# Attention, then two feed-forward layers, under a list planner: a set-back for the attention sums, other staging buffers for the last matrix, two banks for layer one, and a new split of the last units

## The chip, the cores and the metric

The kernel runs on one core of a Trainium2 chip. The metric is the device time of one execution in microseconds (us). The runs shown of the kernel before have a median of 1149.49 us.

## The reference, cut to what matters

```python
scores = (1 / sqrt(64)) * q @ k.T                  # 4 batches, 8 heads, 576 tokens, 64 wide
kth    = 32nd largest score of each row
attn   = softmax(where(scores >= kth, scores, -1e9))
x      = (attn @ v), heads side by side            # 2304 tokens x 512
h      = x @ w_in;  g = max(0.01 * h, h)           # 512 -> 2048
y      = g @ w_out                                 # 2048 -> 512
m      = max(y @ w1, y @ w2, y @ w3)               # 512 -> 768, three times
out    = m @ w_out2                                # 768 -> 512
```

The weight matrices arrive as 64-bit floats, and the kernel turns them into pairs of 16-bit floats on the chip.

## The kernel before, in words

**Numbers.** Every operand of a matmul is kept as a high and a low 16-bit part, so each product is three matmuls (`three`, L873 to L876): high by high, high by low, low by high.

**Attention** (`attention`, L694). There are 72 steps in 20 blocks of up to 128 tokens; a step handles one block for two heads. Its parts, in their order, are: the scores on PE (L716, PSUM tile `s`, a part of `sav`), their copy to SBUF on ACT (L721, tile `S`, three buffers), the 32 largest values of each row on DVE (four MAX8 and three MATCH_REPLACE8 for each head, L736 and L738), the exponential on ACT (L786, `pp`), the mask on DVE and POOL (L791, L795, L798), the split into two 16-bit parts on ACT and POOL (L800, L802, `phl`), one transposing DMA on SP's queue (L805, `pt`), the product with v on PE (L831 to L833, tile `av`, the other part of `sav`), **the attention sums' addition on DVE (L838, `r`)** and their reciprocal (L840), four scaled copies on ACT (L842, `xs`), and the split of the result (`xhl`, L848 and L850). The tiles `pp`, `phl`, `pt`, `xs` and `xhl` have one buffer each. When a block is done, a transposing DMA (L868) puts its tokens into a **token buffer** `xu` (two buffers, handed out strictly in the order in which the program asks for them).

**Feed-forward** (`ffn`, L893). It runs over units of tokens, `UNITS` (L40). A unit can start when the last of its blocks has been attended. It has 672 matmuls of the unit's width: first layer (`h_tile`, L908, tiles `h<-xu,wi`; 16 tiles of 12 matmuls, one bank of the PSUM tag `h` each) and second layer (`acc<-f16t,wo`) interleaved, then the three matrices with their maximum (`h<-k,w`; the maximum is on DVE, L1015), interleaved with the last matrix (`acc<-f16t,w`). The tag `h` has four banks. The planner counts how many a phase may hold: `hH` for layer one, `hM` for the three matrices, `hW` for weight conversion.

**Weights** (`prep_w`, L469). Each chunk is loaded by SP (L484), converted on DVE by three operations for each piece (L498, L501, L504), measured on ACT (L344 or L519), scaled and split on ACT and POOL (L355 to L357). The chunks come in the order `w_in` (8), `w_out` (8), w1 to w3 (6), and the last matrix, called z (4, from `in_w2o`). z's chunks go through the two `raw` buffers, which also carry the loads of q, k and v of batches 1 to 3. A list `ZL` lets q, k and v of batches 2 and 3 wait for the last load of z, and z's loads wait for all q and k loads of batch 1. The conversion of z uses space that the three matrices' conversion used before it. All of z has to be there before the three matrices of unit 0 and before unit 1.

**Order of the work.** The program doesn't write instructions out in order. Each `op` becomes a node with an engine, an estimated duration, a priority `pr` and its dependencies, and `Plan.run` (L123) simulates the five engines: an engine takes the node that can start first, within a tolerance `eps`, and among those the one of lowest `pr`. What each engine executes is that order; on the chip it is fixed, and an instruction whose input is late holds up everything behind it on its engine. A node can start when its inputs are done plus a latency between engines:

```python
m.ready = max(m.ready, end + self.LAT.get((n.eng, m.eng), 0.2))
```

`GATES` (L467) makes chunks 1 and 2 of `w_in` and all chunks of w1 to w3 wait for a write of q of batch 0 to DRAM. `CVX` (L465) adds 0.06 us to the planned duration of a conversion that goes through PSUM.

Of the kernel before, what the change touches and what calls it, by code (L numbers as in the profile page):

```python
# [36 lines left out]
VC = 11  # L37
F0, F1, F2, F3, HB = (0, P), (P, P), (2 * P, P), (3 * P, P), (4 * P, 64)
ORDER = [[F0, HB, F1, F2, F3], [F0, F1, F2, F3, HB], [HB, F0, F1, F2, F3], [F0, F1, F2, F3, HB]]
UNITS = [192, 128] + [256] * 6 + [192, 256]  # L40

PE, ACT, DVE, POOL, SP = "PE", "ACT", "DVE", "POOL", "SP"

# [22 lines left out]


class Node:
    __slots__ = ("eng", "dur", "fn", "pr", "succ", "nd", "ready", "bufs", "eps", "idx", "dma")


class Plan:
# [10 lines left out]
        self.seqs[tag] += 1  # L83
        return b

    def op(self, eng, dur, fn, r=(), w=(), pr=0.0, dma=0.0):
        n = Node()
        n.eng, n.dur, n.fn, n.pr, n.dma = eng, dur, fn, pr, dma
        n.succ, n.ready, n.idx, n.eps = [], 0.0, len(self.nodes), self.eps
        deps, n.bufs = set(), []  # L90
        for k in r:
            if k in self.lastw:
                deps.add(self.lastw[k])
            self.readers.setdefault(k, []).append(n.idx)
        for k in w:
            deps.update(self.readers.get(k, ()))
            if k in self.lastw:
                deps.add(self.lastw[k])
        for k in w:
            self.lastw[k] = n.idx  # L100
            self.readers[k] = []
        deps.discard(n.idx)
        for k in list(r) + list(w):
            k = k[0] if isinstance(k, tuple) else k
            for b in (k, *k.also) if isinstance(k, Buf) else ():
                if b not in n.bufs:
                    n.bufs.append(b)
                    b.left += 1
                    b.emit += 1
        n.nd = len(deps)  # L110
        self.nodes.append(n)
        for d in deps:
            self.nodes[d].succ.append(n)
        return n
# [8 lines left out]
    def run(self):  # L123
        free = {e: 0.0 for e in (PE, ACT, DVE, POOL, SP)}
        dma_free = 0.0
        slots = {t: [0.0] * n for t, n in self.nbufs.items()}
        nexts = {t: 0 for t in self.nbufs}
        pend = {e: [] for e in free}
        order = []
        for n in self.nodes:  # L130
            if n.nd == 0:
                pend[n.eng].append(n)
        total = len(self.nodes)
        while len(order) < total:
            best = None
            for e, lst in pend.items():
                t0 = free[e]
                cand = None
                for n in lst:
                    t, ok = max(n.ready, t0), True  # L140
                    need = {}
                    for b in n.bufs:
                        if b.ap is None and b.last == 0.0 and not getattr(b, "on", False):
                            k = need.get(b.tag, 0)
                            sl = slots[b.tag]
                            if len(sl) <= k or (b.tag not in self.free_order and b.seq != nexts[b.tag] + k):
                                ok = False
                                break
                            need[b.tag] = k + 1
                            t = max(t, sl[k] + 0.2)  # L150
                    if not ok:
                        continue
                    key = (max(t - n.eps, t0), n.pr, n.idx)
                    if cand is None or key < cand[0]:
                        cand = (key, n, t)
                if cand is not None and (best is None or cand[2] < best[2]):
                    best = cand
            if best is None:
                raise RuntimeError("no instruction can go on")
            _, n, t = best  # L160
            pend[n.eng].remove(n)
            for b in n.bufs:
                if not getattr(b, "on", False):
                    b.on = True
                    slots[b.tag].sort()
                    slots[b.tag].pop(0)
                    nexts[b.tag] = max(nexts[b.tag], b.seq + 1)
            free[n.eng] = t + n.dur
            end = t + n.dur
            if n.eng == SP:  # L170
                st = max(t + 1.1, dma_free)
                dma_free = st + n.dma
                end = dma_free + 0.95
            order.append((t, n.idx))
            for b in n.bufs:
                b.left -= 1
                b.last = max(b.last, end)
                if b.left == 0:
                    slots[b.tag].append(b.last)
                    slots[b.tag].sort()  # L180
            for m in n.succ:
                m.nd -= 1
                m.ready = max(m.ready, end + self.LAT.get((n.eng, m.eng), 0.2))
                if m.nd == 0:
                    pend[m.eng].append(m)
        order.sort()
        for _, i in order if self.EMIT else ():
            n = self.nodes[i]
            for b in n.bufs:
                if b.ap is None:  # L190
                    b.ap = b.make()
            n.fn()
            for b in n.bufs:
                b.emit -= 1
                if b.emit == 0 and b.done:
                    b.done()
# [23 lines left out]
def attention_moe_kernel(ctx, tc, qk, v, w_in, w_out, w123, w2o, outT):  # L220
# [8 lines left out]

    NB = {"xu": 2, "raw": 2, "hl": 1, "k2": 7, "kt": 4, "qt": 2, "vt": 4, "S": 3, "w": 1, "m": 2, "nb": 2, "pp": 1,  # L230
          "phl": 1, "pt": 1, "r": 2, "xs": 1, "xhl": 1, "f16t": 4, "yj": 1,
          "s": 1, "av": 1, "acc": 2, "h": 4, "junk": 1, "xcap": 2, "pr": 8, "ph": 4, "ra": 3, "fi": 6, "ft": 9, "rw": 3, "fz": 3, "rc": 2, "hH": 3, "hM": 3, "hW": 1, "kH": 2, "kM": 5, "fH": 2, "fM": 2}
    PSUM_TAGS = ("s", "av", "acc", "h")
    plan = Plan(NB, {"raw", "av", "junk", "hl", "k2", "h", "f16t", "rc"})
    op = plan.op
# [2 lines left out]
    def buf(tag, shape, dt=F32):  # L238
        pl = ps if tag in PSUM_TAGS else sb

        def make():
            cnt[0] += 1
            if tag in ZONE:
                return ZONE[tag].pop(0)
            return pl.tile(shape, dt, tag=tag, bufs=NB[tag], name=f"{tag}_{cnt[0]}")

        b = plan.buf(tag, make)
        if tag in ZONE:
            b.done = lambda: ZONE[tag].append(b.ap)
        return b  # L250
# [106 lines left out]
        op(POOL, pool(n), lambda: G.tensor_tensor(lo(), src(), hi(), op=ALU.subtract), r=r + [w[0]], w=[w[1]], pr=pr)  # L357

    KT, QT, VT, ES = {}, {}, {}, {}
    ZL = [(("w", "z", 3), "ld")]  # L360

    def prep_qk(b, hp, pr, fast):
        d = dr.tile([2, 2, 2, D, S], F16, name=f"dqk{b}_{hp}")
# [96 lines left out]
        VT[b, hp] = t  # L460

    SC = {}
    CVK = "iotz"
    CW = 512
    CVX = 0.06  # L465
    PRW0 = -13.5
    GATES = {1: [("d", 0, 0, 0, 1)], 2: [("d", 0, 1, 0, 1)]}  # L467

    def prep_w(kind, c, parts, hi, lo, colnorm, n2c, s, bi, pr, tags, guard=((), (), []), gate=()):  # L469

# [6 lines left out]
        plan.eps = WEPS  # L477
        for i, saps in enumerate(parts):
            nf = sum(n for _, n in saps)
            f = buf(tags[1], [P, 768 if tags[1] == "raw" else 512], I32)  # L480
            o = 0
            for sap, n in saps:
                raw = buf(tags[0], [P, 768])
                op(SP, 0.55, lambda raw=raw, sap=sap, n=n: Y.dma_start(raw().bitcast(I64)[:, :n], sap),  # L484
                   w=[raw, (key, "ld")] + ([(f, "ld")] if tags[1] in ("raw", "k2") or tags[0] == "raw" else []),
                   r=list(gate) + zr + (zf + [("l1", hp, a) for hp in range(HP) for a in range(2)] * (kind == "z") + guard[2] * (tags[1] == "raw") if kind in "tz" else []), pr=PRW0 if (kind, c) == ("i", 0) else pr,
                   dma=dma(P * n * 8))
                for q in range(0, n, CW):
                    cw = min(CW, n - q)
# [70 lines left out]
    def c1(t, c):  # L560
        return t[:, c:c + 1]
# [25 lines left out]
                ["ZR"] if f < 3 else [("ZF", f - 2)]), gate=GATES[2])  # L587

    def w2_prep(e, pr):
        for hp in range(HP):  # L590
            if (1, hp) not in seen:
                seen.add((1, hp))
                prep_batch(1, hp)
        prep_w("z", e, [[(w2o[e, i], 384) for i in range(2)]], [w2[:, e, 0]], [w2[:, e, 1]],
               None, c1(cz, e), c1(sz, e), c1(bz, e), pr, ("raw", "fz" if e < 3 else "raw"),
               ({0: ["ZB"], 3: [("ZZ", 2)]}.get(e, []), [("ZZ", e - 1)] if e in (1, 2) else [],
                [("ZZ", e - 1)] if e else ["ZB"]))

# [77 lines left out]
        return TE + TS * i if i < NE else TA0 + TA * i  # L676

    EXPP = 4
    COLD = 1.7
    NCOLD = 8  # L680
    FM = 1
# [12 lines left out]
    def attention(i):  # L694
# [141 lines left out]
        nh = 2 if full else 4  # L836
        r = buf("r", [P, 8])
        op(DVE, 0.07, lambda: V.tensor_scalar(r()[:n, 0:nh].rearrange("p (x h) -> p x h", h=2),  # L838
                                             av()[:n, 0:nh // 2, :, 64], 1e-9 * PS, None, op0=ALU.add), r=[avb], w=[(r, 0)], pr=pr)
        op(DVE, 0.08, lambda: V.reciprocal(r()[:n, 4:4 + nh], r()[:n, 0:nh]), r=[(r, 0)], w=[(r, 1)], pr=pr)  # L840
        for h in range(nh):
            op(ACT, act(64, True, 1), lambda h=h: A.activation(xs()[:n, h], avh(h)[:n, 0:64], AF.Copy,  # L842
# [42 lines left out]
                (0, 2))  # L885

    MAXP = 40
    FINP = 40
    CS = 0.8
    DL = 99  # L890
# [2 lines left out]
    def ffn(u, pr0, between=None):  # L893
# [2 lines left out]
        xu = XU[u]  # L896
        xk = [(x, sg[2]) for sg in segs[u] for x in (xu, XC[u])]
        t3 = 3 * mm(N)
        acc, ak, ast, a0 = accs(N)
        clock = [pr0]  # L900

        def tick(t):
# [5 lines left out]
        def h_tile(f):  # L908
            pr = tick(1.3)
            c = f // (FCI // P)  # L910
            p = fbuf("h", "H", [P, 512])
            wk = wkeys("i", [c]) + wkeys("o", range(8)) * (u == 0) + wkeys("z", range(4)) * (u == 1)
            for k in range(KC):
                op(PE, t3, lambda k=k: three(p()[:, :N], lambda x: wi[:, x, k, f * P:(f + 1) * P],
                                             lambda x: xu()[:, x, k, :N], k == 0, k == KC - 1),
# [272 lines left out]
```

## Time and profile before

| what | value |
| --- | --- |
| runs shown, median (lowest to highest) | 1149.49 us (1147.88 to 1154.09), 3 runs |
| the profiled execution's own time | 1152.11 us |
| its span | 1150.2 us |
| mean granted TensorE clock | 0.96 |
| busy: PE, DVE, ACT, POOL | 912.4, 973.6, 757.3, 680.6 us |

The span is that of the program's instructions; 1.9 us of the execution lie around it. A busy share is an average over stages with different limits, so the stretches of the span have to be read apart: up to about 350 us weights are converted beside attention, until about 1050 us attention and feed-forward run side by side, and after that only feed-forward is left.

### The profile page before, as it was taken

What the parts mean: (1) busy time and instruction counts of PE and PEld (TensorE: products, weight loads), DVE (VectorE), ACT (ScalarE), POOL (GpSimd) and SP (SyncE); (2) the same over time, 40 slices, a digit from 0 to 9 for tenths busy, and PEclk for the clock granted to TensorE, in tenths of its full rate; (3) what the DMA queues carried; (4) which work ended last, traced back from release to release, by engine and by line L of the source; (5) the groups of instructions that cost most, each with busy time, mean ns of one, the idle gap of its engine ahead of it and who ended that gap; (6) DMA issues with size and microseconds to landing.
All of it is one profiled execution on the core that took longest, in us unless ns stands there. A gap on an engine that the chain in (4) does not pass through costs nothing.

```text
span 1150.2 us, 27408 instructions
## 1 busy us (share of the span) xinstructions
PE 912.4 (79%) x10294; PEld 797.7 (69%) x10294; DVE 973.6 (85%) x2154; ACT 757.3 (66%) x1625; POOL 680.6 (59%) x1054
## 2 busy tenths in 40 slices
PE   3253246853299799999899989989998998998998
PEld 2131235742199788887688778878887887898987
DVE  3989999989989999999899899899999999995001
ACT  7667747886457767567778665686786666665331
POOL 5555646875446766566777655575787556555231
PEclk9999998975599999999999999999999999999999
DMA  7758455654354423235574333364573433332000
GB/s 234 250 141 264 147 159 166 176 122 134 96 122 88 96 64 83 62 73 131 139 184 118 65 79 70 60 149 78 146 164 66 87 77 52 79 64 52 20 1 19
DMA packets 268549, 125.79 MB, mean 109 GB/s; under 512 B 237440, under 2 KB 255360, under 8 KB 266368
## 3 DMA queue, kind: packets, MB, share of 16 engines
q1 hardware_dynamic: 268416, 124.04, 44.6%
q8 instruction: 81, 1.33, 0.5%
q14 instruction: 52, 0.43, 0.1%
HBM read 62.65 MB, written 14.16 MB: 67 GB/s over the span
## 4 chain that ended last, share of the span: by engine, by line
PE 40%; DMA 14%; DVE 11%; POOL 7%; ACT 6%; issue 5%; SPq 1%; POOLq 0%; ACTq 0%; DVEq 0%
DMA pt<-phl 12%; PE h L874 7%; PE h L875 7%; PE h L876 7%; PE acc L875 4%; DVE m L736 4%; PE acc L874 4%; PE acc L876 4%; DVE w L738 3%; PE sav L716 3%; POOL phl L802 3%; PE sav L831 2%; PE sav L832 2%; PE sav L833 2%; POOL f16t L931 1%
## 5 line engine op out<-in xcount | busy, mean ns | idle before, releaser
L736 DVE MAX8 m<-w 128x8 f32<-128x576 f32 x432 | 309.7, 746 | 0.1
L931 POOL TENSOR_TENSOR f16t<-k,f16t 128x256 f16<-128x256 f32 (+2 forms) x220 | 142.8, 651 | 195.1 <-ACT f16t L925 184.1
L738 DVE MATCH_REPLACE8 w<-m,w 128x576 f32<-128x576 f32 x288 | 211.9, 741 | 0.0
L802 POOL TENSOR_TENSOR phl<-pp,phl 128x576 f16<-128x576 f32 x144 | 183.7, 1281 | 45.5 <-ACT phl L800 43.9
L874 PE MATMUL h<-k,w 128*128 128x256 f16 (+2 forms) x720 | 187.0, 264 | 7.8 <-ACT k L971 5.5
L875 PE MATMUL h<-k,w 128*128 128x256 f16 (+2 forms) x720 | 186.9, 264 | 3.7 <-POOL k L973 3.6
L876 PE MATMUL h<-k,w 128*128 128x256 f16 (+2 forms) x720 | 186.8, 264 | 0.0
L716 PE MATMUL sav<-kt,qt 128*128 128x288 f16 (+5 forms) x800 | 110.1, 288 | 77.1 <-ACT S L721 56.2
L875 PE MATMUL acc<-f16t,wo 128*128 128x256 f16 (+2 forms) x640 | 164.9, 262 | 4.7 <-POOL f16t L931 4.6
L874 PE MATMUL acc<-f16t,wo 128*128 128x256 f16 (+2 forms) x640 | 165.0, 262 | 0.0
L876 PE MATMUL acc<-f16t,wo 128*128 128x256 f16 (+2 forms) x640 | 165.0, 262 | 0.0
L874 PE MATMUL h<-xu,wi 128*128 128x256 f16 (+1 forms) x576 | 155.8, 270 | 5.0 <-ACT k L918 2.2
L876 PE MATMUL h<-xu,wi 128*128 128x256 f16 (+1 forms) x576 | 155.8, 271 | 0.0
L875 PE MATMUL h<-xu,wi 128*128 128x256 f16 (+1 forms) x576 | 155.8, 271 | 0.0
L800 ACT ACTIVATE phl<-pp 128x576 f16<-128x576 f32 x144 | 97.8, 681 | 65.0 <-DMA pt<-phl 27.8
L786 ACT ACTIVATE pp<-S,nb,colt 128x576 f32<-128x576 f32 x144 | 121.5, 860 | 20.6 <-POOL nb L776 12.7
L716 PEld LDWEIGHTS <-qt 128*128 128x128 f16 (+1 forms) x800 | 65.2, 109 | 99.8 <-issue 75.9
L798 POOL TENSOR_TENSOR pp<-pp,S 128x576 f32<-128x576 f32 x72 | 92.2, 1280 | 69.8 <-DVE S L795 42.9
L925 ACT ACTIVATE f16t<-k 128x256 f16<-128x256 f32 (+2 forms) x220 | 85.3, 392 | 59.9 <-DVE k L1015 57.2
L831 PE MATMUL sav<-vt,pt 128*128 128x65 f16 (+1 forms) x800 | 91.2, 202 | 38.5 <-DMA pt<-phl 34.1
L918 ACT ACTIVATE k<-h,colt 128x256 f32<-128x256 f32 (+2 forms) x160 | 71.1, 451 | 70.5 <-PE h L876 69.3
L721 ACT ACTIVATE S<-sav 128x576 f32<-128x576 f32 x144 | 92.8, 644 | 32.2 <-PE sav L716 18.4
(133 smaller groups left out, 2629.5 us busy)
## 6 DMA issues: line engine op xcount, KB each, us to landing
w<-in_w SPq DMA_DIRECT2D x18, 512.0 KB, 3.9
w<-in_w_in SPq DMA_DIRECT2D x8, 1024.0 KB, 6.6
w<-in_w_out SPq DMA_DIRECT2D x8, 1024.0 KB, 4.9
raw<-in_qk SPq DMA_DIRECT2D x24, 288.0 KB, 3.4
dqk<-hl SPq DMA_DIRECT2D x48, 144.0 KB, 2.5
kt<-dqk SPq DMA_DIRECT2D x16, 288.0 KB, 3.3
qt<-dqk SPq DMA_DIRECT2D x144, 32.0 KB, 2.2
raw<-in_v SPq DMA_DIRECT2D x12, 352.0 KB, 3.5
```

Of the source, the lines that this page charges most:

```text
L716: T.matmul(p()[osl, h, o:o + w], q()[:, hh, st, :n], k()[:, hh, kc:kc + w], start=st == 0, stop=st == 1, skip_group_check=True)
L721: op(ACT, act(S, True), lambda t=t, p=p: A.activation(t().rearrange("p (a s) -> p a s", a=2), p()[:, :, :288], AF.Copy), r=[p], w=[(Sp, j) ...
L736: op(DVE, dve(S) * 1.03, lambda mc=mc, src=src: V.max(mc(), src()), r=rd, w=[(m, j, 0, r)], pr=pd)
L738: op(DVE, dve(S) * 1.03 + 0.06, lambda mc=mc, src=src, j=j: V.match_replace(out=wj(j), in_to_replace=mc(), in_values=src(), imm_value=NEG) ...
L786: op(ACT, act(S, aps=2), lambda j=j, es=es: A.activation(pp()[:, j], Sb[j](), AF.Exp, bias=nb()[:, j:j + 1], scale=es[:, 0:1]), r=[(Sp, j) ...
L800: op(ACT, act(S), lambda j=j: A.activation(phl()[:, 0, j], pp()[:, j], AF.Copy), r=[(pp, j)], w=[(phl, 0, j)], pr=pr)
L802: op(POOL, pool(S), lambda j=j: G.tensor_tensor(phl()[:, 1, j], pp()[:, j], phl()[:, 0, j], op=ALU.subtract), r=[(pp, j), (phl, 0, j)], w= ...
L831: T.matmul(o, hc, vh, start=c == 0, stop=False, skip_group_check=True)
L874: T.matmul(out, wt(0), xt(0), start=first, stop=False, skip_group_check=True)
L875: T.matmul(out, wt(0), xt(1), start=False, stop=False, skip_group_check=True)
L876: T.matmul(out, wt(1), xt(0), start=False, stop=last, skip_group_check=True)
L931: op(POOL, pool(N) + 0.044, lambda: G.tensor_tensor(hl()[:, 1, :N], g()[:, 0, :N], hl()[:, 0, :N], op=ALU.subtract), r=[(g, 0), (hl, 0)], ...
```

## The change

The sum's addition (L838) gets a `lag` of 3.0 us: the planner takes its input to be ready 3.0 us later than it computes, and so puts it further back in DVE's order. Nothing waits on the chip for that time. The last matrix is staged through the token buffers `xu` and no longer through `raw`; the two rules that tied it to the loads of q, k and v (`ZL`, `l1`) go. `hH` becomes 2. The last two units are 256 and 192 tokens wide and no longer 192 and 256. Chunk 1 of `w_in` isn't gated any more (chunk 0 was not), and `CVX` becomes 0. `PRE` and `G1` are added in a form that changes nothing.

```diff
-UNITS = [192, 128] + [256] * 6 + [192, 256]
+UNITS = [192, 128] + [256] * 7 + [192]
...
-                m.ready = max(m.ready, end + self.LAT.get((n.eng, m.eng), 0.2))
+                m.ready = max(m.ready, end + self.LAT.get((n.eng, m.eng), 0.2) + m.lag)
...
-          ... "hH": 3, "hM": 3, "hW": 1, ...
+          ... "hH": 2, "hM": 3, "hW": 1, ...
...
-    ZL = [(("w", "z", 3), "ld")]
+    ZL = []
...
+    ZT = "xu"
...
-    CVX = 0.06
+    CVX = 0.0
...
-    GATES = {1: [("d", 0, 0, 0, 1)], 2: [("d", 0, 1, 0, 1)]}
+    GATES = {1: [], 2: [("d", 0, 1, 0, 1)]}
...
-                   w=[raw, (key, "ld")] + ([(f, "ld")] if tags[1] in ("raw", "k2") or tags[0] == "raw" else []),
+                   w=([(f, "ld")] if tags[1] in ("raw", "xu", "k2") or tags[0] in ("raw", "xu") else []) + [raw, (key, "ld")],
...
     def w2_prep(e, pr):
-        for hp in range(HP):
+        for hp in range(HP) if ZT == "raw" else ():
...
-               None, c1(cz, e), c1(sz, e), c1(bz, e), pr, ("raw", "fz" if e < 3 else "raw"),
+               None, c1(cz, e), c1(sz, e), c1(bz, e), pr, (ZT, "fz" if e < 3 else ZT),
...
+    RLAG = 3.0
...
         op(DVE, 0.07, lambda: V.tensor_scalar(r()[:n, 0:nh].rearrange("p (x h) -> p x h", h=2),
-                                             av()[:n, 0:nh // 2, :, 64], 1e-9 * PS, None, op0=ALU.add), r=[avb], w=[(r, 0)], pr=pr)
+                                             av()[:n, 0:nh // 2, :, 64], 1e-9 * PS, None, op0=ALU.add), r=[avb], w=[(r, 0)], pr=pr, lag=RLAG)
```

## Rows read from the trace of the kernel before

**Rows 1.** The page, the span in 40 slices: busy tenths of PE and DVE.

```profile
PE   3253246853299799999899989989998998998998
...
DVE  3989999989989999999899899899999999995001
```

**Rows 2.** Windows: stretch, then busy us (instructions) of PE, PEld, DVE, ACT, POOL; clock, DMA.

```profile
50.00:350.00 300.00, 153.91 (x1685) 128.09 (x1683) 278.30 (x609) 205.96 (x391) 177.92 (x256) 0.85 0.55 149
350.00:1050.00 700.00, 649.46 (x7607) 574.61 (x7605) 654.38 (x1452) 484.20 (x1091) 450.43 (x678) 1.00 0.44 94
```

**Rows 3.** Waits of DVE over the whole span: total us, times, longest.

```profile
DVE r L838 <- PE sav L833: 40.7, 37, 2.8
DVE k L1015 <- PE h L876: 35.9, 28, 3.5
...
DVE r L838 <- PE sav L716: 9.6, 6, 2.3
```

**Rows 4.** Waits of DVE in the window 0 to 350 us.

```profile
DVE r L838 <- PE sav L833: 8.8, 8, 2.2
...
DVE r L838 <- PE sav L716: 4.2, 2, 2.2
```

**Rows 5.** Timeline of DVE: one wait at 522 us, the last at 1060 us.

```profile
522.90 0.16 DVE L838 TENSOR_SCALAR r<-sav 128x2 f32<-128x2 f32 x1 [1.04 <-PE sav L833]
...
1060.73 0.15 DVE L838 TENSOR_SCALAR r<-sav 64x4 f32<-64x4 f32 x1 [2.84 <-PE sav L833]
```

**Rows 6.** Waits of PE in the window 350 to 1050 us.

```profile
PE sav L831 <- DMA pt<-phl: 17.3, 22, 1.6
PE sav L716 <- ACT S L721: 11.1, 15, 1.6
```

**Rows 7.** Windows of the last two units: from unit 8's first matmul, and from unit 9's.

```profile
996.30:1070.00 73.70, 69.31 (x966) 66.09 (x967) 54.52 (x126) 41.97 (x113) 39.72 (x64) 1.00 0.29 63
1070.00:1146.20 76.20, 74.23 (x676) 65.76 (x673) 5.96 (x13) 25.34 (x60) 18.86 (x33) 1.00 0.02 7
```

**Rows 8.** Timeline of PE, matmuls of 192 and 256 columns, and SP's last token transpose.

```profile
999.97 0.25 PE L874 MATMUL h<-xu,wi 128*128 128x192 f16 x1
...
1000.96 0.25 PE L874 MATMUL h<-xu,wi 128*128 128x192 f16 x1
...
1063.63 1.19 SPq L868 DMA_TRANSPOSE xu<-xhl  x1
...
1145.19 0.27 PE L876 MATMUL acc<-f16t,w 128*128 128x256 f16 x1
...
1145.84 0.27 PE L876 MATMUL acc<-f16t,w 128*128 128x256 f16 x1
```

**Rows 9.** Timelines of PE and ACT: a layer-one tile and the eviction two tiles before.

```profile
185.02 0.25 PE L874 MATMUL h<-xu,wi 128*128 128x192 f16 x1
...
190.69 0.40 ACT L918 ACTIVATE k<-h,colt 128x192 f32<-128x192 f32 x1
...
1005.16 0.25 PE L874 MATMUL h<-xu,wi 128*128 128x192 f16 x1
...
1005.07 0.73 ACT L918 ACTIVATE k<-h,colt 128x192 f32<-128x192 f32 x2
```

**Rows 10.** Window between unit 0's second layer and its three matrices, columns as in Rows 2.

```profile
246.50:316.50 70.00, 21.33 (x209) 15.66 (x210) 65.92 (x149) 40.62 (x85) 38.02 (x56) 0.52 0.47 120
```

**Rows 11.** Timelines of SP and POOL: z's first loads, z's last split, unit 2's tokens.

```profile
255.11 7.55 SPq L484 DMA_DIRECT2D raw<-in_w2o  x3
...
313.78 1.65 POOL L357 TENSOR_TENSOR w<-raw,w 128x768 f16<-128x768 f32 x1 [2.12 <-ACT w L356]
...
321.10 1.26 SPq L868 DMA_TRANSPOSE xu<-xhl  x1
```

**Rows 12.** Timeline of DVE, the first 26 us.

```profile
9.77 1.29 DVE L498 TENSOR_SCALAR acc<-w 128x512 int32<-128x512 int32 x2 [1.80 <-DMA w<-in_w_in]
...
23.01 0.42 DVE L530 TENSOR_REDUCE colt<-h 128x1 f32<-128x256 f32 x1 [4.17 <-PE h L525]
```

More of the change, by code (lines that the diff above doesn't have):

```diff
@@ L68 @@
 class Node:
-    __slots__ = ("eng", "dur", "fn", "pr", "succ", "nd", "ready", "bufs", "eps", "idx", "dma")
+    __slots__ = ("eng", "dur", "fn", "pr", "succ", "nd", "ready", "bufs", "eps", "idx", "dma", "lag")
 class Plan:
@@ L84, in buf, with op @@
         return b
-    def op(self, eng, dur, fn, r=(), w=(), pr=0.0, dma=0.0):
+    def op(self, eng, dur, fn, r=(), w=(), pr=0.0, dma=0.0, lag=0.0):
         n = Node()
-        n.eng, n.dur, n.fn, n.pr, n.dma = eng, dur, fn, pr, dma
+        n.eng, n.dur, n.fn, n.pr, n.dma, n.lag = eng, dur, fn, pr, dma, lag
         n.succ, n.ready, n.idx, n.eps = [], 0.0, len(self.nodes), self.eps
@@ L231, in attention_moe_kernel @@
           "phl": 1, "pt": 1, "r": 2, "xs": 1, "xhl": 1, "f16t": 4, "yj": 1,
-          "s": 1, "av": 1, "acc": 2, "h": 4, "junk": 1, "xcap": 2, "pr": 8, "ph": 4, "ra": 3, "fi": 6, "ft": 9, "rw": 3, "fz": 3, "rc": 2, "hH": 3, "hM": 3, "hW": 1, "kH": 2, "kM": 5, "fH": 2, "fM": 2}
+          "s": 1, "av": 1, "acc": 2, "h": 4, "junk": 1, "xcap": 2, "pr": 8, "ph": 4, "ra": 3, "fi": 6, "ft": 9, "rw": 3, "fz": 3, "rc": 2, "hH": 2, "hM": 3, "hW": 1, "kH": 2, "kM": 5, "fH": 2, "fM": 2}
     PSUM_TAGS = ("s", "av", "acc", "h")
@@ L462, in attention_moe_kernel @@
     SC = {}
+    ZT = "xu"
     CVK = "iotz"
     CW = 512
-    CVX = 0.06
+    CVX = 0.0
     PRW0 = -13.5
-    GATES = {1: [("d", 0, 0, 0, 1)], 2: [("d", 0, 1, 0, 1)]}
+    GATES = {1: [], 2: [("d", 0, 0, 0, 1)]}
     def prep_w(kind, c, parts, hi, lo, colnorm, n2c, s, bi, pr, tags, guard=((), (), []), gate=()):
@@ L479, in prep_w @@
             nf = sum(n for _, n in saps)
-            f = buf(tags[1], [P, 768 if tags[1] == "raw" else 512], I32)
+            f = buf(tags[1], [P, 768 if tags[1] in ("raw", "xu") else 512], I32)
             o = 0
@@ L484, in prep_w @@
                 op(SP, 0.55, lambda raw=raw, sap=sap, n=n: Y.dma_start(raw().bitcast(I64)[:, :n], sap),
-                   w=[raw, (key, "ld")] + ([(f, "ld")] if tags[1] in ("raw", "k2") or tags[0] == "raw" else []),
-                   r=list(gate) + zr + (zf + [("l1", hp, a) for hp in range(HP) for a in range(2)] * (kind == "z") + guard[2] * (tags[1] == "raw") if kind in "tz" else []), pr=PRW0 if (kind, c) == ("i", 0) else pr,
+                   w=([(f, "ld")] if tags[1] in ("raw", "xu", "k2") or tags[0] in ("raw", "xu") else []) + [raw, (key, "ld")],
+                   r=list(gate) + zr + (zf + [("l1", hp, a) for hp in range(HP) for a in range(2)] * (kind == "z" and ZT == "raw") + guard[2] * (tags[1] in ("raw", "xu")) if kind in "tz" else []), pr=PRW0 if (kind, c) == ("i", 0) else pr,
                    dma=dma(P * n * 8))
@@ L887, in attention_moe_kernel @@
     MAXP = 40
+    G1 = 4
+    PRE = {}
     FINP = 40
@@ L898, in ffn @@
         t3 = 3 * mm(N)
-        acc, ak, ast, a0 = accs(N)
+        acc, ak, ast, a0 = PRE.pop(u, None) or accs(N)
+        if u == 0 and G1 == 0:
+            PRE[1] = accs(UNITS[1])
         clock = [pr0]
@@ L911, in h_tile @@
             p = fbuf("h", "H", [P, 512])
-            wk = wkeys("i", [c]) + wkeys("o", range(8)) * (u == 0) + wkeys("z", range(4)) * (u == 1)
+            wk = wkeys("i", [c]) + wkeys("o", range(8)) * (u == 0) + wkeys("z", range(G1)) * (u == 1)
             for k in range(KC):
```

## The prediction, made before any run of the change

> **What bounds the kernel now.** I read the page's slices first, then the windows, then who waits for whom on DVE and on PE, then the end. In the slices [rows 1] the reader is to see two engines that are full in different places: DVE from the start until shortly before the end, PE only from the middle on. The windows make numbers of it [rows 2]. From 50 to 350 us PE works 153.9 of 300 us and DVE 278.3: DVE is the bound there. From 350 to 1050 us DVE works 654.4 of 700 us and PE 649.5, so DVE has 45.6 us left and PE 50.5. There both are near their limit, and neither can gain much more than the other allows.
>
> So I look at where DVE's idle time comes from. The waits of DVE [rows 3] have one line on top that is no work at all: the attention sums' addition waits for PE, 40.7 us in 37 waits and 9.6 us in 6, together 50.3 us, the longest 2.8. Its own run takes 0.16 us [rows 5]. DVE works in order; while it stands at this instruction, the MAX8 and MATCH_REPLACE8 of later steps stand behind it. 13.0 of the 50.3 us lie before 350 us [rows 4], the rest after. The last wait, 2.8 us at 1060 us [rows 5], comes after DVE's last mask and holds up nothing, so 47.5 us are at stake, 13.0 before 350 us and 34.5 after.
>
> The end: unit 9 runs alone, from 1070.0 to 1146.1 us [rows 7, 8], and 4.1 us later the span ends at 1150.2. Its last tokens were issued at 1063.6 us [rows 8], so it started 6 us after that, in the moment in which unit 8 was through. Attention and PE reach the end together.
>
> **The change part by part.** The sum is made against the profiled execution, 1152.1 us; the median of the runs shown is 2.6 us lower, and I subtract that at the end.
>
> **The set-back, L838.** It adds and removes no instruction; it moves one of 0.16 us behind DVE work of 3.0 us, some four MAX8 or MATCH_REPLACE8. Since the longest wait was 2.8 us, every one of them would be covered if all else stayed. The bounds are a gain of 47.5 us and a loss of 3 us (the sums come later, and a unit's tokens with them; the very last have nothing to be put behind). I don't take the full gain, because of PE. Before 350 us PE has room, and I take 9 of the 13. After 350 us PE can give at most the 50.5 us that it is idle. Of these, 17.3 us are waits for the transposed probabilities and 11.1 us for the copy of the scores [rows 6]; such waits follow from PE's own fixed order, the change doesn't touch them, and I let them stay. That leaves some 22 us, and as some of these are gaps at a unit's start I take 19 of the 34.5. Sum: **28 us**. What is late next is the transposed probabilities: PE will stand at L831 more often, and DVE at its maximum L1015, which waits for PE.
>
> **The last units, 256 and 192.** Unit 8 ends with the block that it ended with before (tokens 1856 to 2112 end in the same block as 1856 to 2048), so it starts no later, and 64 tokens move from unit 9 into it. Twelve matmuls of 192 columns take 0.99 us, 0.083 each, and six of 256 take 0.65 us, 0.108 each [rows 8]; 672 times the difference is 17 us. Unit 9 falls from 76.2 to some 59 us, and unit 8 grows from 73.7 to some 91 us. PE was idle 4.4 of the 73.7 us [rows 7], so a longer unit 8 can swallow at most that. PE's work is the same; it ends later with unit 8 and is quicker with unit 9. Bounds 0 to 4.4 us; I take **2 us**, in the middle, since unit 9's start still hangs on both.
>
> **Two banks for layer one.** With three banks PE may be two tiles ahead of ACT, with two banks one. Tile 2 of unit 0 began at 185.02 us, and the bank of tile 0 was free only at 190.69 plus 0.40 us [rows 9]: with two banks PE would have stood 6.1 us there. I went through all 140 pairs of a tile and the eviction two tiles before; 13 overlapped, the first this one, the last that of unit 8, where tile 5 began at 1005.16 and tile 3's eviction at 1005.07 [rows 9]. They sum to 30.6 us, 26.3 in unit 0, 3.9 in unit 1, 0.4 in all the others. What unit 0 loses is hidden: PE then waits for z, and from 246.5 to 316.5 us it is busy for only 21.3 of 70 us [rows 10], so 48.7 us of cover stand against 26.3. Without that cover it would cost 26 us. Taken as **0**, bounds 0 to 31. The Trainium skill says the opposite of such a cut (Perfetto Trace Analysis, section Matmul Optimizations: make sure that all eight PSUM banks are used); all eight stay allocated here, but by that rule PE would lose time in every unit, as in the third rival below, whose price is worked out there from rows.
>
> **z through the token buffers.** Loads, conversions and splits are the same in number. z can't start before the conversion of the three matrices is over, whichever buffer it uses, and its first load is issued at 255.1 us [rows 11]; two `raw` buffers become two `xu` buffers, of which unit 0 gives its one back with layer one. So z's pace stays. New is that unit 2's tokens queue behind nine staging buffers: z's last split ended at 315.4 us and unit 2's first transpose was issued at 321.1 [rows 11]. If z came over 5.7 us later, that transpose would hold up SP's queue, and the next transposes of probabilities behind it. On the other side the loads of q, k and v are free of z. Taken as **0**, bounds 6 us either way.
>
> **Gates and planned durations.** Chunk 1 of `w_in` can be loaded while DVE still idles at the start, where one wait alone is 4.2 us before 23.0 us [rows 12]. A chunk's six conversions are three pairs like the first, 1.29 us, so 3.9 us could move there. Its load goes past q and k in SP's queue and shares their engines, which may delay the first step by about as much. **1 us** of gain, bounds 4 either way. `CVX` changes orders alone; its cost is within these bounds.
>
> Sum: 28 + 2 + 0 + 0 + 1 = 31 us, so 1152.1 - 31 = 1121.1 us for such an execution, and 2.6 less for the median: **1119 us** in round numbers.
>
> **The rivals.**
>
> *The next wait takes over after 350 us.* `pp`, `phl` and `pt` have one buffer each, and both engines are near full there. If each us that the addition no longer waits is waited at L831, at L1015 or for the scores instead, the 19 us go and the 9 us before 350 us, 2 and 1 stay: about **1137 us**. For it speaks that PE's waits for the probabilities are already 22 [rows 6]; against it that PE has 22 us which no row of attention claims.
>
> *The change doesn't do what it says.* The planner puts everything else into another order too. If the additions are again met too early, because DVE runs ahead of the plan by more than 3 us, the 50 us stay and only small terms are left: about **1149 us**. Against it speaks that no wait was longer than 2.8 us.
>
> *Slower: two banks hold PE in every unit.* Place: layer one of units 1 to 9. If attention gets denser, ACT's evictions trail as in unit 0, and PE stands at each start of a tile. Unit 1 lost 3.9 us at tiles of 128 columns; twice that for tiles of twice the length is 7.8 us a unit, 62 us over the eight units after it, less the 31 us gained: about **1180 us**. It decides from some 4 us a unit on, where it eats the gain. Against it: 0.4 us for all units after 1 in the trace before.
>
> **How the numbers follow.** Forecast 0.58, next wait 0.22, no effect 0.12, slower by the banks 0.08. The forecast's own range is 1100 (all of the 47.5 us but a few) to 1131 us (half of the gain after 350 us lost). The range to 1146 us takes in the next wait and the better half of no effect; what is left out is the rest of that, the banks, and a gain beyond 1100. A measurement of this kernel tells about 0.5% from no change, here 5.7 us. Faster by more than that: the forecast, nearly all of the next wait, a little of no effect, 0.80. Within it: the rest of these, 0.11. Slower: the banks and a bad order, 0.09.
>
> **What would show it.** In the profile after: the additions' rows among DVE's waits fall from 50.3 us below 15; DVE's busy time between 350 us and the end of attention comes above 96% of the window (93.5% before); the last token transpose is issued near 1036 us and not at 1063.6; unit 9's 672 matmuls take about 59 us, unit 8's some 90; PE's waits for ACT's eviction at L918 stay at a few us after unit 1; unit 2's first token transpose doesn't wait for z. I am wrong if the additions wait as long as before, if PE waits in their place, or if DVE is filled and the end doesn't move, which would make PE the only bound.

## The result, and the profile after

The changed kernel takes 1131.7 us (median of 4 runs, 1129.44 to 1134.74) where the kernel before takes 1151.79 us beside it (4 runs): ratio 0.9841, 95% interval 0.9808 to 0.9874. The forecast was 1119 us, range 1100 to 1146. The profiled execution after took 1129.44 us, its span is 1127.3 us: 22.9 less than the 1150.2 of before.

One correction to the section on the change: the diff printed there, and its words, leave the gate of chunk 2 and of the three matrices `w1` to `w3` as it was. In the kernel that ran it changes too: `GATES = {1: [], 2: [("d", 0, 0, 0, 1)]}`, so that these loads wait for pair 0's q and no longer for pair 1's.

Lines shift by 2 (L838 is L840 now, L716 L718, L868 L870) and later by 6 (L1015 is L1021). First the slices of the page after, as in [rows 1]:

```profile
PE   2253236764798998998879899989999998999998
...
DVE  3999999999899999999999899899999999995101
```

The shape is that of before: DVE full from the start, PE from the middle. Next the windows after, columns as in [rows 2]: the two of [rows 2], then the time up to unit 3's first matmul (475.40 us) and from there to PE's last.

```profile
50.00:350.00 300.00, 176.34 (x2007) 149.20 (x2007) 286.25 (x633) 220.24 (x432) 192.98 (x284) 0.86 0.57 151
350.00:1050.00 700.00, 655.10 (x7421) 573.45 (x7419) 646.50 (x1434) 478.06 (x1065) 452.17 (x662) 0.99 0.43 93
...
0.00:475.40 475.40, 306.55 (x3510) 262.31 (x3511) 438.64 (x971) 334.95 (x679) 292.96 (x469) 0.91 0.55 145
475.40:1123.30 647.90, 610.50 (x6784) 538.60 (x6781) 534.24 (x1184) 421.40 (x946) 394.17 (x586) 0.99 0.39 87
```

The same two stretches of the kernel before, cut at its own unit 3 (495.40 us):

```profile
0.00:495.40 495.40, 303.54 (x3508) 260.42 (x3509) 446.63 (x987) 339.42 (x686) 295.68 (x471) 0.91 0.53 141
495.40:1146.10 650.70, 608.81 (x6788) 537.29 (x6787) 526.94 (x1168) 416.87 (x937) 384.89 (x583) 1.00 0.39 85
```

On PE **20.0 us come before unit 3 starts** (495.4 to 475.4) and **2.8 us after it** (650.7 to 647.9). That is a cut of PE's progress alone. A unit also needs its own last tokens from attention, and cut by these the picture is another one. SP's timelines show the last transposes for unit 3 and for unit 7, before and then after:

```profile
475.05 1.24 SPq L868 DMA_TRANSPOSE xu<-xhl  x1
...
895.44 1.26 SPq L868 DMA_TRANSPOSE xu<-xhl  x1
```

```profile
469.99 1.31 SPq L870 DMA_TRANSPOSE xu<-xhl  x1
...
876.89 1.23 SPq L870 DMA_TRANSPOSE xu<-xhl  x1
```

They land at 477.8 and 898.3 us before, at 472.8 and 879.6 after. So unit 3's tokens are 5.0 us earlier and unit 7's 18.7. Unit 3 starts 17.6 us behind its tokens before and 2.6 after; unit 7, at 900.7 and 881.0, 2.4 and 1.4 behind. What PE is late by at unit 3 in the kernel before, it has made up by unit 7: the 20 us at unit 3 are not by themselves the gain at the end.

Attention runs on DVE, so here are DVE's windows, cut at the landing of unit 3's tokens and at the end of DVE's last MAX8 (1046.5 us before, 1025.2 after), before and then after:

```profile
0.00:477.80 477.80, 285.94 (x3324) 244.60 (x3325) 429.39 (x949) 330.56 (x669) 289.11 (x463) 0.91 0.53 143
477.80:1046.50 568.70, 529.00 (x5952) 464.67 (x5951) 532.03 (x1176) 392.49 (x871) 364.10 (x548) 1.00 0.45 98
```

```profile
0.00:472.80 472.80, 303.95 (x3464) 259.85 (x3465) 436.05 (x965) 334.50 (x677) 291.58 (x466) 0.91 0.55 146
472.80:1025.20 552.40, 517.38 (x5717) 450.49 (x5716) 523.30 (x1157) 385.83 (x850) 365.58 (x533) 0.99 0.45 99
```

DVE is idle for 48.4 and 36.7 us before, together 85.1, and for 36.8 and 29.1 after, together 65.9. That is 11.6 us saved early and 7.6 late, of the 22.9 by which the span fell. The forecast had 10 us early (9 from the set-back, 1 from the gates) and 21 late.

The waits of DVE after, over the whole span, the rows of the addition [rows 3]:

```profile
DVE r L840 <- PE sav L718: 15.0, 14, 2.7
...
DVE r L840 <- ACT S L723: 7.0, 8, 2.2
...
DVE r L840 <- PE sav L835: 3.2, 1, 3.2
...
DVE r L840 <- ACT k L924: 1.3, 1, 1.3
```

They sum to 26.5 us, against 52.4 before: beside the two rows of [rows 3], 50.3 us, stands a third, which the prediction left out:

```profile
DVE r L838 <- ACT S L721: 2.1, 2, 1.1
```

By the set-back's reasoning that is 26 us of DVE. It looks like the cause; the experiments show that the set-back isn't what took these waits away.

The end, windows of units 8 and 9 [rows 7]:

```profile
977.40:1063.90 86.50, 84.38 (x952) 74.79 (x953) 55.86 (x124) 44.88 (x111) 44.31 (x62) 1.00 0.23 53
1063.90:1123.50 59.60, 57.65 (x687) 56.72 (x687) 5.48 (x15) 22.66 (x61) 16.23 (x35) 1.00 0.03 11
```

And SP's timeline after, against [rows 11]: the last load of `w1` to `w3`, z's first load, unit 2's first and last token transpose.

```profile
215.52 0.38 SPq L485 DMA_DIRECT2D w<-in_w  x1
...
224.48 6.73 SPq L485 DMA_DIRECT2D xu<-in_w2o  x2
...
316.94 1.23 SPq L870 DMA_TRANSPOSE xu<-xhl  x1
...
372.99 2.14 SPq L870 DMA_TRANSPOSE xu<-xhl  x1
```

In the kernel before the last of `w1` to `w3` was issued 31 us later:

```profile
246.29 0.57 SPq L484 DMA_DIRECT2D w<-in_w  x1
```

### The profile page after: what moved, and what is told of

Same layout as the page of the kernel before. It is cut to its first block, busy times and chain, and to the rows that moved or that the text cites. A ratio compares the mean times of both kernels' runs of the same rounds, so it can differ in the third digit from the quotient of the medians.

```text
span 1127.3 us, 27415 instructions
## 1 busy us (share of the span) xinstructions
PE 917.1 (81%) x10292; PEld 800.9 (71%) x10292; DVE 972.9 (86%) x2154; ACT 757.2 (67%) x1625; POOL 687.1 (61%) x1054
## 4 chain that ended last, share of the span: by engine, by line
PE 47%; DVE 16%; ACT 11%; DMA 10%; POOL 7%; issue 6%; SPq 1%; POOLq 0%; ACTq 0%; DVEq 0%
PE h L876 8%; PE h L877 8%; PE h L878 8%; DMA pt<-phl 6%; PE acc L877 5%; PE acc L876 5%; PE acc L878 5%; PE sav L718 4%; DVE m L738 4%; DVE w L740 3%; ACT S L723 2%; PE sav L833 2%; PE sav L834 2%; PE sav L835 2%; DVE w L505 2%
## 5 line engine op out<-in xcount | busy, mean ns | idle before, releaser
L877 PE MATMUL acc<-f16t,wo 128*128 128x256 f16 (+2 forms) x640 | 167.0, 265 | 5.3 <-POOL f16t L937 5.0
L876 PE MATMUL acc<-f16t,wo 128*128 128x256 f16 (+2 forms) x640 | 166.9, 265 | 0.9 <-ACT k L974 0.5
L878 PE MATMUL acc<-f16t,wo 128*128 128x256 f16 (+2 forms) x640 | 166.9, 265 | 0.0
L718 PE MATMUL sav<-kt,qt 128*128 128x288 f16 (+5 forms) x800 | 109.7, 288 | 61.9 <-ACT S L723 45.9
L718 PEld LDWEIGHTS <-qt 128*128 128x128 f16 (+1 forms) x800 | 64.7, 109 | 87.3 <-issue 71.7
L924 ACT ACTIVATE k<-h,colt 128x256 f32<-128x256 f32 (+2 forms) x160 | 71.0, 451 | 64.1 <-PE h L878 63.8
```

What stands on the lines that cost most here:

```text
L718: T.matmul(p()[osl, h, o:o + w], q()[:, hh, st, :n], k()[:, hh, kc:kc + w], start=st == 0, stop=st == 1, skip_group_check=True)
L876: T.matmul(out, wt(0), xt(0), start=first, stop=False, skip_group_check=True)
L877: T.matmul(out, wt(0), xt(1), start=False, stop=False, skip_group_check=True)
L878: T.matmul(out, wt(1), xt(0), start=False, stop=last, skip_group_check=True)
```

## The experiments

Three theories are weighed. The prediction's (A): the set-back makes the gain, by waits taken from DVE. The rival (B): the other edits, or the order into which they together bring the plan, make it, and the additions' waits follow. The third (C) came up after the first runs: unit 0's three matrices start earlier (their first matmul, "M" below, moved from 316.8 to 295.0 us), and the end moves with M. Two more, E and F, are told where they are tried. Each ratio is to the kernel before on the same chip, with its 95% interval; two kernels are compared by their ratios.

### The set-back taken out, and the set-back alone

```diff
# a_nolag: the changed kernel with
-    RLAG = 3.0
+    RLAG = 0.0
# b_lag: the kernel before with Node.lag and
+    ..., w=[(r, 0)], pr=pr, lag=3.0)
```

> The changed kernel with the set-back of the sums' addition taken out (lag 0), all else of the change kept. Theory A (the set-back is the main term): DVE's waits at the addition come back to 45 to 55 us, the last token transpose is issued some 12 us later, and the time is 1143 to 1150 us. Theory B (the other edits and the new order they cause made the gain, the additions would wait less in any other order): the waits stay below 35 us and the time is 1130 to 1137 us.

> The kernel before with the set-back of 3.0 us alone. Theory A: the waits at the addition fall from 50 us to below 30, the time is 1133 to 1140 us. Theory B: within 5 us of the kernel before, 1145 to 1155 us, because PE or another wait takes the place.

Without the set-back the changed kernel is **faster**: 1122.21 us (4 runs, 1119.43 to 1123.73), ratio 0.9766 (0.9741 to 0.9791), an interval wholly below that of the change: 27 us faster than the kernel before, more than either theory expected. This is the best kernel of the study. Alone on the kernel before, the set-back gives 1143.99 us, ratio 0.9965 (0.9947 to 0.9983), some 4 us. The waits of DVE in a_nolag, whole span:

```profile
DVE r L840 <- PE sav L835: 21.5, 28, 3.4
...
DVE r L840 <- PE sav L718: 4.4, 4, 2.2
...
DVE r L840 <- ACT S L723: 1.6, 3, 0.8
...
DVE r L840 <- ACT phl L802: 0.3, 1, 0.3
```

That is 27.8 us, where the changed kernel with its set-back has 26.5 and the kernel before 52.4. So the waits halve without anything being set back. The waits of DVE in b_lag, whole span:

```profile
DVE k L1015 <- PE h L876: 39.6, 32, 4.7
...
DVE r L838 <- PE sav L716: 9.4, 9, 1.8
DVE r L838 <- ACT S L721: 9.2, 11, 1.7
DVE pp L791 <- ACT pp L786: 7.3, 6, 3.0
...
DVE r L838 <- ACT k L918: 2.4, 1, 2.4
```

Here the additions' waits do fall, from 52.4 to 21.0 us, but the time falls by only 4 to 5: other rows grow, the maximum L1015 from 35.9 [rows 3] to 39.6, and `pp` from 0.6 to 7.3.

### The addition moved back with every other order kept

In these kernels an edit re-plans everything, so b_lag doesn't show what moving the addition does. b_back6 does: it takes the planned order of the kernel before on PE, ACT, POOL and SP as it is, and moves only the addition behind 5 more of DVE's planned operations (in 65 of 72 steps; in the others as far as can be) and its reciprocal with it.

```diff
+    order = self.set_back(order, 6)   # DVE's list alone; PE, ACT, POOL, SP keep theirs
```

> The kernel before with its own order kept on PE, ACT, POOL and SP, and on DVE the sums' addition and reciprocal of each step moved behind five more DVE instructions (65 of 72 steps; fewer in seven, where less was possible), about 3.5 us of DVE work; the planner does not plan anew. The prediction's main term, undisturbed by a new order: the waits at the addition fall from 50 us below 15 and the time falls by 20 us or more, to 1120 to 1131 us. If those waits are only where DVE happens to meet the pace that the other engines' orders set: the waits go and return at other instructions, and the time stays within 6 us, 1143 to 1152 us.

1299.56 us (5 runs), ratio 1.1307 (1.1282 to 1.1331): **150 us slower**. DVE's waits (its lines are 68 to 70 further down: the addition is L906, the maximum L1085, `pp` L859):

```profile
DVE colt L397 <- PE acc L1050: 67.7, 10, 46.6
DVE k L1085 <- PE h L946: 60.0, 41, 4.2
DVE pp L859 <- ACT pp L854: 48.7, 26, 3.8
...
DVE r L906 <- PE sav L784: 11.6, 10, 3.5
...
DVE r L906 <- PE sav L901: 5.0, 4, 2.8
```

The additions wait 16.6 us, about as wanted. (The first row was 49.0 before; 46.6 of it are one wait in both kernels.) Neither forecast allowed for such a loss. ACT's waits show who needed them, first b_back6, then before:

```profile
ACT xs L912 <- DVE r L909: 192.4, 69, 5.4
```

```profile
ACT xs L842 <- DVE r L840: 21.7, 16, 2.9
```

ACT scales the sums by the reciprocal, in order; its 16 waits of 21.7 us have become 69 of 192.4. One of them on the timelines of DVE and of ACT, where the last bracket is the idle time before an instruction:

```profile
529.09 0.16 DVE L909 RECIPROCAL r<-r 128x2 f32<-128x2 f32 x1
...
529.34 0.52 ACT L912 ACTIVATE xs<-sav,r 128x64 f32<-128x64 f32 x2 [2.93 <-DVE r L909]
```

Behind that scaled copy stand, on ACT, the split, the copy of the scores L789 and the split of the probabilities L868; they come late, PE gets its inputs late, and DVE waits for both. PE's waits for that copy of the scores show it, b_back6 and then before:

```profile
PE sav L784 <- ACT S L789: 124.5, 57, 9.6
```

```profile
PE sav L716 <- ACT S L721: 56.2, 37, 9.2
```

The place of the addition is tied to ACT's order: it can only move if ACT's copies move too, and then it is another plan.

### The last units

```diff
# a_units: the changed kernel with the split of before; b_units: before with
-UNITS = [192, 128] + [256] * 6 + [192, 256]
+UNITS = [192, 128] + [256] * 7 + [192]
```

> The changed kernel with the last units 192 and 256 as before. If the split of the units gave the 8 us by which the span fell more than the last token transpose moved (22.9 against 14.6 us): 1138 to 1143 us, with unit 9 alone at the end for 76 us. If it gave only the 2 us of the prediction: 1132 to 1135 us.

> The kernel before with the last units 256 and 192 alone. By the prediction's sum 0 to 4 us of gain, 1146 to 1152 us, because unit 8's 17 us more stand against unit 9's 17 us less. If PE has slack that the longer unit 8 fills: a gain of 8 us or more, 1140 to 1144 us.

a_units 1133.64 us, ratio 0.9871 (0.9846 to 0.9895), against 0.9841 for the change; b_units 1148.51 us, ratio 0.9994 (0.9979 to 1.001). Two readings of 1 to 3 us, neither outside the intervals: the forecast's 2 us fits, 0 isn't excluded.

### The last matrix in the token buffers

```diff
# b_z: before with ZT = "xu" and ZL = [], and the lines that go with them
# a_zraw: the changed kernel with
-    ZL = []
+    ZL = [(("w", "z", 3), "ld")]
...
-    ZT = "xu"
+    ZT = "raw"
```

> The kernel before with the last matrix staged in the token buffers alone (and the two rules that tied it to the loads of q, k and v gone). Theory C (what counts is when unit 0's three matrices can start, that is when the last matrix is ready; from there to PE's last matmul the six kernels so far took 820 to 831 us): they start 15 us or more before 316.8 us, at 300 or earlier, and the time falls by as much, to 1130 to 1137 us. Theory A (waits at the sums' addition) and my prediction's term of 0 for this part: no change, 1146 to 1152 us.

> The changed kernel with the last matrix back in the raw buffers, behind the loads of q and k of batch 1. Theory C: unit 0's three matrices start at 312 us or later and the time is 1145 to 1152 us. Prediction's term of 0: 1129 to 1135 us.

Alone it makes the kernel slower: 1157.41 us, ratio 1.0048 (1.0026 to 1.007). Undone in the changed kernel it also makes it slower, by 6 us: 1137.65 us, ratio 0.9892 (0.9867 to 0.9918; its interval just touches that of the change). The same edit costs 6 us alone and gains 6 in company, each at the bound that the prediction gave; both expectations missed, in both runs. In a_zraw z's first load follows the last of `w1` to `w3` by 21 us (215.2, 236.3), in the change by 9.

### Two banks for layer one

```diff
# a_hh3: the changed kernel with "hH": 3; b_hh2: before with
-"hH": 3
+"hH": 2
```

> The changed kernel with three banks for layer one again. Theory E (with two banks, unit 0's layer one leaves PSUM banks to the conversion of the three matrices, whose loads end at 215 us in the changed kernel and at 246 in the one before; so the last matrix is ready earlier and PE isn't behind its plan in units 0 to 2): the last load of the three matrices is issued at 235 us or later, unit 0's three matrices start at 308 us or later, unit 3 starts after 485 us (475 in the changed kernel) and the time is 1140 to 1150 us. Theory F (the gates and planned durations did it): the last load near 215 us, 1127 to 1136 us.

> The kernel before with two banks for layer one alone. Theory E: the last load of the three matrices is issued before 230 us, unit 0's three matrices start at 295 to 305 us and not at 317, the waits at the sums' addition fall with it though nothing is set back, and the time is 1130 to 1140 us. Theory F: 1146 to 1152 us, or slower.

Alone it is worth nothing: 1149.76 us, ratio 0.9992 (0.9973 to 1.0011), as forecast; undone in the changed kernel it costs 7 to 8 us: 1139.58 us, ratio 0.9905 (0.988 to 0.9929). In b_hh2 theory E had the early loads right and the time wrong, F the time right. In a_hh3 E had the loads wrong (the last is issued at 217.8 us) and the time at its edge, F the loads right and the time wrong. In b_hh2 two things move, one each way. SP's timeline shows the last load of `w1` to `w3` 25 us earlier than in the kernel before, and the last token transpose of unit 2 late (issued 383.83, in the kernel before 376.0):

```profile
221.10 0.37 SPq L484 DMA_DIRECT2D w<-in_w  x1
...
383.83 3.32 SPq L868 DMA_TRANSPOSE xu<-xhl  x1
```

M came 14 us earlier, at 302.4, but unit 3 only 3 us earlier, at 492.3 us. That the late tokens ate the rest is likely, but not shown. As for the loads: in all runs of the changed kernel the last one is issued by 217.8 us, also with three banks or with the old gates (213.0); alone, two banks bring it to 221.1, while the set-back, the units and the last matrix leave it at 240 to 246. So two banks are enough to bring it forward, but not needed in company.

The Trainium skill says to make sure that all eight PSUM banks are used (Perfetto Trace Analysis, section Matmul Optimizations). No run here tests that rule, since all eight stay allocated. That a smaller cap for layer one makes PE wait for evictions is not seen in the changed kernel, where PE waits for L924 for 0.8 us in all:

```profile
PE h L876 <- ACT k L924: 0.8, 3, 0.4
```

### The gates and the planned durations

```diff
# a_gatecvx: the changed kernel with both lines of before
-    CVX = 0.0
+    CVX = 0.06
...
-    GATES = {1: [], 2: [("d", 0, 0, 0, 1)]}
+    GATES = {1: [("d", 0, 0, 0, 1)], 2: [("d", 0, 1, 0, 1)]}
```

> The changed kernel with the gates of the weight loads and the 0.06 us of planned conversion time as before. Theory E: the last load of the three matrices stays near 215 to 222 us and the time within 5 us of the changed kernel, 1127 to 1137 us. Theory F: it moves towards 246 us, and the time is 1140 to 1150 us.

1145.95 us, ratio 0.9965 (0.9947 to 0.9982): without this edit more than three quarters of the gain are gone. Theory F had that time right, but not its reason: the last of these loads is issued at 213.0 us and not near 246. And unit 3 starts at 476.7 us, 1.3 later than in the change. The loss lies after it; the window from there to PE's last matmul:

```profile
476.70:1140.80 664.10, 619.85 (x6826) 544.07 (x6825) 532.91 (x1192) 425.27 (x946) 393.04 (x588) 0.98 0.39 85
```

That is 16.2 us more than the 647.9 of the change, from an edit of loads that are over some 250 us before. a_mfree, below, shows the same figure. The reverse, this edit alone on the kernel before, wasn't run, nor the gates and `CVX` apart from each other.

### The start of unit 0's three matrices, earlier and later

```diff
# a_mfree: unit 0's three matrices don't wait for z
-            wk = wkeys("t", [f]) + (wkeys("t", range(NF2)) + wkeys("z", range(4))) * (u == 0)
+            wk = wkeys("t", [f]) + wkeys("t", range(NF2)) * (u == 0)
# a_zcap: z's loads one at a time, each after the one before is converted
+                if kind == "z":
+                    raw.also = (plan.buf("zc", lambda: 1),)      # NB: "zc": 1
```

> The changed kernel, but unit 0's three matrices no longer wait for the last matrix (only its own product does). Theory C in its strong form (PE's start there sets the end): they start 10 us or more before 295 us and the time falls by some 10 us, to 1118 to 1125 us. If unit 1, which still waits for the last matrix, or attention sets the pace: 1129 to 1134 us.

> The changed kernel with the loads of the last matrix one at a time (a cap of one staging buffer for its halves), the same work otherwise. Theory C: the matrix is ready some 5 to 20 us later, unit 0's three matrices start as much later than 295 us, and the time grows by the same number of us. Theory A: no change, 1129 to 1134 us.

a_zcap starts M 9.4 us later (304.4) and unit 3 11.4 us later (486.8), and PE ends 11 us later: 1140.09 us, ratio 0.9921 (0.9891 to 0.9951). That fits theory C. a_mfree starts M 38 us earlier (257.2) and by theory C's strong form should win some 10 us; it takes 1142.1 us, ratio 0.9929 (0.9905 to 0.9953), slower than the change, which neither forecast had. Its window from unit 3's first matmul on, and from SP's timeline the last token transpose of unit 2:

```profile
477.00:1141.10 664.10, 619.20 (x6826) 543.35 (x6825) 533.45 (x1192) 425.31 (x946) 392.80 (x588) 0.98 0.39 85
```

```profile
375.87 1.23 SPq L870 DMA_TRANSPOSE xu<-xhl  x1
```

First, M no longer decides: unit 1 is through at 356.1 us, but unit 2 starts at 380.2 all the same, since its last tokens land at 379.7 us (377.1 in the change). Unit 3 starts 2.7 us after its own last tokens land, in the change 2.6: with these tokens, an earlier M can't bring it forward by more than that. Second, the late stretch is again 664.1 us. From 480 us on a_mfree and a_gatecvx run the same 1183 DVE instructions in the same order, and on PE, ACT and POOL too the same instructions in the same order; the change shares about half of the DVE sequence with them. So the loss goes with the order, which both edits happen to bring about. Its size is less sure than two equal figures suggest: each is one execution, that of a_mfree 5.1 us above its kernel's median, that of the change 2.3 below. By the ratios a_mfree loses 10 us against the change and a_gatecvx 14.

### What all the runs give together

Times in us from the span's start: M, the landing of unit 2's and of unit 3's last tokens, unit 3's first matmul; then the rest from there to PE's last matmul, and DVE's idle time up to the end of its last MAX8. Each row is one profiled execution.

| kernel | M | tokens 2 | tokens 3 | unit 3 | rest | DVE idle |
|---|---|---|---|---|---|---|
| before | 316.8 | 378.7 | 477.8 | 495.4 | 650.7 | 85.1 |
| b_units | 315.1 | 377.0 | 474.6 | 492.3 | 651.1 | 83.4 |
| b_z | 314.3 | 386.2 | 477.0 | 495.6 | 655.8 | 90.7 |
| b_lag | 310.1 | 378.6 | 476.8 | 492.4 | 646.1 | 77.1 |
| b_hh2 | 302.4 | 389.4 | 481.6 | 492.3 | 648.6 | 82.3 |
| a_zcap | 304.4 | 379.0 | 475.1 | 486.8 | 647.5 | 76.1 |
| a_zraw | 300.9 | 374.3 | 471.7 | 479.8 | 652.3 | 69.9 |
| a_nolag | 298.3 | 378.9 | 469.5 | 474.4 | 643.5 | 63.2 |
| a_hh3 | 297.7 | 375.0 | 476.8 | 479.8 | 654.3 | 76.5 |
| a_gatecvx | 295.6 | 382.0 | 474.0 | 476.7 | 664.1 | 85.9 |
| **the change** | 295.0 | 377.1 | 472.8 | 475.4 | 647.9 | 65.9 |
| a_units | 293.5 | 375.2 | 472.5 | 475.1 | 649.3 | 65.3 |
| a_mfree | 257.2 | 379.7 | 474.3 | 477.0 | 664.1 | 87.9 |

**Unit 3's start.** In 11 of the 13 it follows M by 176 to 182 us. The windows from M to unit 3, before and in the change:

```profile
316.80:495.40 178.60, 166.35 (x2172) 153.22 (x2170) 165.32 (x374) 118.39 (x280) 104.58 (x162) 0.99 0.41 86
```

```profile
295.00:475.40 180.40, 168.72 (x2209) 154.24 (x2207) 168.95 (x380) 115.71 (x273) 106.28 (x163) 0.99 0.37 79
```

PE is busy 93% of both, and DVE 93 and 94%, so the windows alone don't tell which of the two sets the pace. The unit's own tokens help: unit 3 starts 15 to 19 us after they land in before, b_units, b_z and b_lag, where PE has fallen behind, and 2.6 to 3.0 us after in the change, a_units, a_gatecvx, a_mfree and a_hh3. So unit 3's start is about the later of two dates, M and 180 us, or its own tokens and 2.6 us; in the change both fall together (475.0 and 475.4). b_hh2 fits neither, by some 8 us.

**The end.** It follows another figure. In all 13 kernels DVE works 956 to 964 us up to its last MAX8, and the span is its idle time up to there plus 1057 to 1066 us (in b_back6, idle 223.7 us, plus 1071). The span ends 98 to 106 us after that MAX8 in every one: attention, on DVE, sets the end. The kernel that leaves DVE idle least, a_nolag, is the fastest, and the change saves 19.2 of its 22.9 us there. Neither M nor the additions' waits stand for that idle time: a_gatecvx has M of the change and the idle time of before, and b_lag has 31 us less of the additions' waits than before, but only 8 us less idle time.

## Why the prediction was right or wrong

The time lies in the range and the sign is right, but by luck: the step that carries 28 of the 31 us, **the set-back, failed**. The edits that were put at 3 us in all give 27 us without it (a_nolag); with it the change gains 18 by its ratio (20 by the medians), so here it costs some 9. The set-back was costed with DVE alone: every wait "covered if all else stayed", and bounds of a gain of 47.5 us and a loss of 3. With all else kept the loss is 150 us (b_back6). What the step left out is who waits for the addition: ACT's scaled copies, 192.4 us for 21.7. Re-planned, so that ACT moves along, the set-back is worth some 4 us alone and less than nothing here. The waits at the addition read as a symptom: they tell that the product with v came late by PE's and ACT's orders, and fall to 27.8 us in a_nolag, where nothing is set back.

What held of the prediction's frame: DVE's idle time is the thing to save. It was right to start there, and wrong on how the idle time would be taken away.

**"z can't start before the conversion of the three matrices is over", so its pace stays**: the sentence held (z follows the last of these loads by 9 us, before and after), the conclusion didn't. The loads of `w1` to `w3` themselves came 31 us earlier, which no step costed, and z with them, so M moved by 21.8 us and unit 3 by 20.0. How much of that reached the end isn't shown: unit 3's tokens came only 5.0 us earlier, a_zcap, with M 9.4 us later, ends 11 us later, but a_mfree, with M 38 us earlier, ends later too. The bounds of 6 us either way held, once at each end.

**Two banks, 0**: right alone. But the cover that was named, PE's idle time before M, isn't fixed: the edit alone moves the loads by 25 us and M by 14. Undone in the changed kernel it costs 7 to 8 us, which the 0 doesn't have. The third rival, slower by the banks, fell.

**Gates, 1 us, bounds 4**: the early part agrees (1.3 us at unit 3). But only chunk 1's gate was priced, while that of chunk 2 and of `w1` to `w3` changed as well. And that "its cost is within these bounds" is wrong: undone, gates and `CVX` together cost 14 us, and the late stretch shows 16.2.

**The last units, 2 us**: fits. Unit 9 takes 59.6 us (59 forecast), unit 8 86.5 until unit 9 starts (some 90).

**The rivals.** "The next wait takes over after 350 us" (1137 us) describes b_lag best, where most of what the additions no longer wait is waited elsewhere. In the change the additions' waits fall by 26 us and DVE's idle time by 19. "The change doesn't do what it says" fell, since the waits did fall.

**The marks.** The additions wait 26.5 us, not below 15. DVE is busy 95.0% from 350 us to its last mask (641.94 of 675.8 us), not above 96%. The last token transpose is issued at 1049.0 us, not near 1036. PE's waits for the eviction are 0.8 us, as marked. Unit 2's first transpose is free of z, as marked: it is issued at 316.94 us, and z's last split began at 292.50.

**What stays open.** Which edit makes the gain: the change with any one of its five parts undone (gates and `CVX` as one) still has unit 3 at 474 to 480 us, while none of the four parts tried alone on the kernel before brings it below 492, and the fifth, gates and `CVX`, wasn't tried alone. It is the largest when undone (14 us), so it is the first to try. And what makes one late order take 643.5 us and another 664.1: that it goes with the order was seen in two kernels with the same one, not what in it costs the time. With such scatter, the 9 us by which a_nolag wins may be its order's luck as much as the set-back's absence.

## What to carry to other kernels

Before an instruction on an in-order engine is moved back because it waits, look up who waits for its result and price that engine's queue; a wait for an operand can be the mark of another engine's order. Where a planner lays out every engine, an edit's effect is its own plus that of a new order, here 10 to 14 us from edits of loads and waits that lie hundreds of us earlier: change one edit with the order held, or don't credit a few us to it. Sum the idle time of the engine that is full, up to its last piece of the work that sets the end: here that sum follows the time in every run, and one row of waits doesn't. Look for the dates that set a stage's start (here M and the tokens) and ask of each edit, also of those costed at nothing, which of them it moves.

## What was not expected of the hardware

Runs of the kernel before differ in the mean granted clock of TensorE without being slower for it: 1145.91 us at 0.955 and 1145.97 at 0.916. Of the 23 runs beside a_nolag, 13 have 0.910 to 0.918 and a median of 1148.0 us, 10 have 0.949 to 0.965 and a median of 1149.9. The page of b_hh2, itself a run at 0.913, shows where the lower mean comes from:

```profile
PEclk9975557785699999999999999999999999999999
```

and that of the change:

```profile
PEclk9999996875799999999999999999999999999999
```

A slice is some 28 us; a tenth of 5 is the lower of the two levels, 1.2 GHz, nearly all through it. The clock is low only in slices before some 315 us, where DVE is nearly full and PE has room [rows 2], and at nine tenths or more from there on; so the lower level costs nothing there that the time shows.
